# Taking the last row of the last expert's w2 past the slot outputs, straight into the output tiles

## The chip, the cores and the metric

The kernel runs on one core of a Trainium2 chip. The metric is the device time of one execution in microseconds (us). Before the change the median of three runs was 121.67 us (121.21 to 122.52).

## The reference, cut to what matters

The program is a linear attention with decay (the RWKV step), followed by a soft mixture of experts: every expert works on four "slots", each a weighted mean of all 3072 tokens, and every token gets back a weighted mean of the 32 slot outputs. The change lies in the second half:

```
logits = x @ phi                                  # 3072 x 32
d = exp(logits - max over tokens);  d /= sum over tokens
slot_input = (d.T @ x).reshape(E, S_per_e, D)     # E = 8, S_per_e = 4, D = 384
for e in range(E):
    h = maximum(slot_input[e] @ w1[e], 0)         # 4 x 1024
    slot_out[e] = h @ w2[e]                       # w2[e]: 1024 x 384
c = exp(logits - max over slots);  c /= sum over slots
out = c @ slot_out                                # 3072 x 384
```

The kernel leaves out the maxima, uses one table of exponentials for both softmaxes, and divides late: by `csr` (one over a slot's sum over the tokens) in the slot outputs, by `rsr` (one over a token's sum over the slots) in the output tiles.

## The kernel before, in words

**The attention** (lines 128 to 575) takes up the first 90 us of the trace. Its loop over 32 pieces also sends off the weights, under GpSimd's queue: `load_w` (lines 133 to 139) loads the eight experts' w1, then the eight w2, with a cast from float32 to bf16. `W_AT` says at which piece which load is issued. The last expert's w2 comes in three loads after the loop (lines 576, 577): rows y = 0 to 3, rows 4 to 6, row 7. A "row" y is a slab of 128 x 384: w2 is laid out as `(p y) d -> p y d`, so slab y holds the rows 8p + y of the matrix, one on each partition p.

**The experts' first layer** (lines 614 to 631) leaves relu(slot_input @ w1) in `h_sb`, for two groups g of four experts; an expert's slots are in a block of 32 rows of its own, 96 to 127 for the last one. Lines 646 to 650 transpose that to `hT`. **The second layer** is `second(g, experts)`: for each slab y, each half x of the 384 columns and each expert, one product of 128 x 32 weights with 128 x 192 of w2, added up in the two PSUM banks `SO` (Xb and Yb). TensorE runs it in the order in which w2 arrives: all of group 0, the first two experts of group 1, one filler product (`busy(1)`), then the last expert but one, then the last expert. `row_sums` (line 635) makes the tokens' sums, a product with one column for each tile, and `row_recip` (line 640) inverts them on VectorE. Then lines 671 and 672 scale the two halves of the slot outputs into `so`, one on VectorE, one on ScalarE.

**The output** (lines 675 to 704) is 24 tiles of 128 tokens x 384. `emit` makes a tile with one product, `LexpT` (the table of exponentials, slots on partitions, columns of the tile 24 apart) times `so`, and evicts it with a scaling by `rsr`, on VectorE for even tiles and ScalarE for odd ones; tiles 0 and 1 are made in two halves, one on each engine. The tiles use six PSUM banks in turn (`ob`: T1, T0, Ab0, Vb, Xb, Yb). They leave in nine transfers of `sizes = [1, 1, 2, 2, 2, 4, 4, 4, 4]` tiles. Transfers 0, 1, 2, 4, 6 and 8 are issued by SyncE (SP), transfers 3, 5 and 7 by GpSimd (POOL):

```
O((sp, pool)[gi % 2 if gi > 1 else 0].dma_start(out=out_v[:, i0:i, :], in_=o_s))
```

Each engine runs its instructions in the order of the program text (`O` keeps it). So TensorE does nothing for the output before the last slab of the last expert is in and `so` is scaled.

Of the kernel before, what the change touches and what calls it, by code (L numbers as in the profile page):

```python
# [9 lines left out]
def kernel(  # L10
# [14 lines left out]
    C = 128  # L25
    nC = S // C
    Nn, Dm = out.shape
    ES = moe_phi.shape[1]
    E = moe_w1.shape[0]
# [3 lines left out]
    nF = F // C  # L33
# [5 lines left out]
    nN = Nn // C  # L39
# [6 lines left out]
    f32 = mybir.dt.float32  # L46
    bf = mybir.dt.bfloat16
    i32 = mybir.dt.int32
    AF = mybir.ActivationFunctionType
    ALU = mybir.AluOpType  # L50

    def O(ins):
        return tc.keep_in_program_order(ins)

    pe, dve, act, pool, sp = nc.tensor, nc.vector, nc.scalar, nc.gpsimd, nc.sync

    big = ctx.enter_context(tc.tile_pool(name="big", bufs=1))
    cst = ctx.enter_context(tc.tile_pool(name="cst", bufs=1))
# [6 lines left out]
    EG = E // 2  # L65
    raw = [big.tile([128, 3 * RW], f32, name=f"raw{j}") for j in range(NR)]
    eW2 = nF * Dm
    w1_all = big.tile([128, E, nM, F], bf, name="w1_all")

    def w2_of(e):  # L70
        g, j = divmod(e, EG)
        return raw[1 + g][:].bitcast(bf)[:, j * eW2:(j + 1) * eW2].rearrange("p (y d) -> p y d", y=nF)
# [4 lines left out]
    T0 = psb.tile([128, 1024], bf, name="T0")  # L77
    T1 = psb.tile([128, 1024], bf, name="T1")
    Ab = psb.tile([128, 2, 512], f32, name="Ab")
# [13 lines left out]
    LexpT = cst.tile([128, Nn], bf, name="LexpT")  # L93
# [39 lines left out]
    def load_w(n, y0=0, y1=nF):  # L133
        if n < E:
            O(pool.dma_start(out=w1_all[:, n, :, :],
                             in_=moe_w1[n].rearrange("(p mo) f -> p mo f", p=128)))
        else:
            O(pool.dma_start(out=w2_of(n - E)[:, y0:y1, :],  # L138
                             in_=moe_w2[n - E].rearrange("(p y) d -> p y d", p=128)[:, y0:y1, :]))

    def keep_warm(n, bank=Yb, data=None):
        data = warm if data is None else data
        for _ in range(n):
            O(pe.matmul(bank[:, 0:512], data[:, 0:128], data[:, 0:512], start=True, stop=True))  # L144
# [349 lines left out]
    for i in range(-5, nH):  # L494
# [50 lines left out]
        if i in Z_AT:  # L545
            q = Z_AT[i]
# [12 lines left out]
        if i == 6:  # L559
            for mi in range(nM):  # L560
                for j in range(nM):
# [4 lines left out]
                                start=(j == 0), stop=(j == nM - 1)))  # L566
# [6 lines left out]
            load_w(nw)  # L573
            nw += 1
    assert nw == 2 * E - 1
    for y0, y1 in ((0, 4), (4, 7), (7, 8)):
        load_w(nw, y0, y1)


# [2 lines left out]
    Ab0 = Ab[:, 0, :]  # L582

    def busy(n):
        keep_warm(n, Ab[:, 1, :], w1_all[:, 0, 0, :])
# [23 lines left out]
    csr = cst.tile([128, 1], f32, name="csr")  # L609
# [4 lines left out]
    hb = [[Ab0, Vb[:]], [Yb[:], Ab[:, 1, :]]]  # L614
    FH = F // 2
    PH = C // 2
    h_sb = [Wf[0].bitcast(bf)[:, g * F:(g + 1) * F].rearrange("p (y c) -> p y c", c=C) for g in range(2)]
    hT = [Wf[1].bitcast(bf)[:, g * F:(g + 1) * F].rearrange("p (y c) -> p y c", c=C) for g in range(2)]
    for g in range(2):
        for a in range(2):  # L620
            for mi in range(nM):
                for j in range(EG):
                    O(pe.matmul(hb[g][a][32 * j:32 * j + 32, 0:FH], uns[:, mi, g, j, :],
                                w1_all[:, g * EG + j, mi, a * FH:(a + 1) * FH],
                                start=(mi == 0), stop=(mi == nM - 1), skip_group_check=True))
            src = hb[g][a][:, 0:FH].rearrange("p (q y) -> p y q", y=nF)
            dst = h_sb[g][:, :, a * PH:(a + 1) * PH]
            if a == 0:
                O(act.activation(out=dst, in_=src, func=AF.Relu))
            else:  # L630
                O(dve.tensor_scalar(out=dst, in0=src, scalar1=0.0, scalar2=None, op0=ALU.max))

    rsr = cst.tile([128, nN], f32, name="rsr")

    def row_sums(a, z):
        for i in range(a, z):
            O(pe.matmul(Mb[:, i:i + 1], LexpT[:, i:Nn:nN], ones[:, 0:1],
                        start=(i == a), stop=(i == z - 1), skip_group_check=True))

    def row_recip(a, z):  # L640
        O(dve.reciprocal(rsr[:, a:z], Mb[:, a:z]))

    HD = Dm // 2
    NY = nF // 2
    tb = [[T0[:], T1[:]], [Ab0.bitcast(bf), Vb[:].bitcast(bf)]]
    for g in range(2):
        for y in range(nF):
            O(pe.transpose(tb[g][y // NY][:, (y % NY) * C:(y % NY + 1) * C], h_sb[g][:, y, :], ident[:]))
        O(act.copy(hT[g][:, 0:NY, :].rearrange("p y c -> p (y c)"), tb[g][0][:, 0:NY * C]))
        O(dve.tensor_copy(hT[g][:, NY:nF, :].rearrange("p y c -> p (y c)"), tb[g][1][:, 0:NY * C]))  # L650
        if g == 0:
            row_sums(0, 8)
    row_recip(0, 8)
    SO = [Xb[:, 0:HD], Yb[:, 0:HD]]

    def second(g, experts):
        for y in range(nF):
            for x in range(2):
                for j in experts:
                    O(pe.matmul(SO[x][32 * j:32 * j + 32, :], hT[g][:, y, 32 * j:32 * j + 32],  # L660
                                w2_of(g * EG + j)[:, y, x * HD:(x + 1) * HD],
                                start=(g == 0 and y == 0), stop=(g == 1 and y == nF - 1), skip_group_check=True))

    second(0, range(EG))
    second(1, range(EG - 2))
    busy(1)
    second(1, (EG - 2,))
    second(1, (EG - 1,))
    row_sums(8, 12)
    so = Wf[1].bitcast(bf)[:, 2 * F + nM * ES * 8:2 * F + nM * ES * 8 + Dm]  # L670
    O(dve.tensor_scalar_mul(so[:, 0:HD], SO[0], csr[:, 0:1]))
# [7 lines left out]
             Wf[0][:, 2 * Dm:4 * Dm]]  # L679
            + [raw[0][:, x * 4 * Dm:(x + 1) * 4 * Dm] for x in range(4)])  # L680

    def emit(i, bank, dst, x0, x1, eng):
        op = ob[bank % 6][:, 0:x1 - x0]
        O(pe.matmul(op, LexpT[:, i:Nn:nN], so[:, x0:x1], start=True, stop=True))
        if eng is dve:
            O(dve.tensor_scalar_mul(dst[:, x0:x1], op, rsr[:, i:i + 1]))  # L686
        else:
            O(act.activation(out=dst[:, x0:x1], in_=op, func=AF.Copy, scale=rsr[:, i:i + 1]))

    i = 0  # L690
    for gi, sz in enumerate(sizes):
        o_s = obuf[gi][:, 0:sz * Dm].rearrange("p (n m) -> p n m", m=Dm)
        i0 = i
        for j in range(sz):
            if i < 2:
                emit(i, 2 * i, o_s[:, j, :], 0, HD, dve)
                emit(i, 2 * i + 1, o_s[:, j, :], HD, Dm, act)
            else:
                emit(i, i + 2, o_s[:, j, :], 0, Dm, (dve, act)[i % 2])
            i += 1  # L700
            if i in (6, 12):
                row_sums(i + 6, i + 12)
                row_recip(i + 6, i + 12)
        O((sp, pool)[gi % 2 if gi > 1 else 0].dma_start(out=out_v[:, i0:i, :], in_=o_s))  # L704
# [30 lines left out]
```

The softmax here doesn't subtract the row's maximum and nothing guards it: scores larger than these inputs give would overflow.

## Time and profile before

| | |
|---|---|
| median of three runs | 121.67 us (121.21 to 122.52) |
| the profiled execution, its time | 121.55 us |
| the profiled execution, its span | 119.8 us |
| mean granted TensorE clock | 0.959 |
| busy: TensorE, VectorE, ScalarE, GpSimd | 102.0, 96.4, 83.9, 59.2 us |
| last piece of w2 on chip | 103.1 us |
| first output transfer issued | 104.74 us |
| last output eviction done | 110.87 us |
| output data stops moving | 117.5 us |

How to read it: the span is what the profile covers, 1.75 us less than the time of the same execution. A time "at 103.1 us" is counted from the start of the span. The profile's page gives busy time by engine, the span in 40 slices, the transfers by queue (q0: those that GpSimd issues, q1: those of SP and ScalarE), and the chain of work that ended last. The timeline lists instructions with their start, duration, engine, line, output and inputs; `SPq` and `POOLq` are the engines' instruction sequencers, and "issue to landing" is the time from a transfer's instruction to its completion.

### The profile page before, as it was taken

The page shows a single profiled execution, that of the slowest core. Times are in us where ns is not written, and L with a number is a line of the kernel's source. Part 1 is how long each engine was busy: PE and PEld are TensorE (multiplying, and loading weights), DVE is VectorE, ACT ScalarE, POOL GpSimd, SP SyncE. Part 2 cuts the span into 40 slices and gives each one's busy share as a digit, 9 for nine tenths or more (in the row PEclk, how much of TensorE's full clock was granted, in tenths as well). Part 3 has the DMA queues.
Part 4 walks back from the last instruction along what each step waited for, and adds up shares of the span by engine and source line. Part 5 has one row for each costly group of instructions (what it writes and reads, how often), then busy time and mean ns, then how long its engine had stood idle before and what let it go on. Part 6 is the DMA issues. An engine that isn't in the chain of part 4 may idle for free.

```text
span 119.8 us, 4336 instructions
## 1 busy us (share of the span) xinstructions
PE 102.0 (85%) x1797; PEld 82.0 (68%) x1797; DVE 96.4 (81%) x187; ACT 83.9 (70%) x183; POOL 59.2 (49%) x70
## 2 busy tenths in 40 slices
PE   5994977799999999999999999999998998896000
PEld 1453866687888888889878798888785696683000
DVE  6899999999999999899999899999954420399000
ACT  4459769797988898988988997998882520398000
POOL 7328634599999999788677595011000000013000
PEclk9998699999999999999999999999999999999955
DMA  2999999999999999999999999999999998179992
GB/s 83 255 370 374 373 367 369 363 391 367 339 381 385 348 229 215 213 213 217 213 217 213 217 218 215 212 217 212 217 215 217 211 209 161 23 274 383 410 410 99
DMA packets 20925, 31.79 MB, mean 265 GB/s; under 512 B 1129, under 2 KB 17898, under 8 KB 20906
## 3 DMA queue, kind: packets, MB, share of 16 engines
q0 software_dynamic: 2960, 14.55, 55.5%
q1 hardware_dynamic: 17920, 16.96, 41.8%
q8 instruction: 14, 0.23, 0.7%
q14 instruction: 5, 0.04, 0.1%
q10 hardware_dynamic: 26, 0.00, 0.0%
HBM read 39.38 MB, written 4.72 MB: 368 GB/s over the span
## 4 chain that ended last, share of the span: by engine, by line
DMA 34%; PE 28%; DVE 17%; issue 6%; ACT 3%; POOL 3%; POOLq 0%; DVEq 0%; ACTq 0%
DMA raw<-in_moe_w_dram 34%; PE Vb L284 4%; PE T L235 3%; DVE W L188 3%; DVE prod L257 3%; PE Ab L299 3%; PE Yb L352 2%; POOL kr L228 2%; DVE AT L304 2%; PE T L247 2%; PE Mb L325 2%; DVE kn L252 2%; DVE Z L341 2%; PE Yb L144 2%; PE Yb L365 1%
## 5 line engine op out<-in xcount | busy, mean ns | idle before, releaser
L228 POOL TENSOR_TENSOR kr<-raw,W 128x576 bf16<-128x576 f32 x30 | 42.2, 1428 | 13.8 <-ACT W L192 6.2
L304 DVE TENSOR_TENSOR AT<-Ab,mask_ut 128x768 bf16<-128x768 f32 x32 | 30.3, 946 | 0.8 <-PE Ab L299 0.6
L235 PE MATMUL T<-ident,kr 128*128 128x128 bf16 x192 | 16.8, 227 | 1.8 <-POOL kr L228 1.7
L284 PE MATMUL Vb<-v_bf,Q 128*128 128x96 bf16 x288 | 17.8, 208 | 0.0
L284 PEld LDWEIGHTS <-Q 128*128 128x128 bf16 x288 | 15.9, 99 | 1.5 <-issue 0.2
L241 ACT COPY kT<-T 128x768 bf16<-128x768 bf16 x16 | 12.8, 800 | 4.6 <-PE T L235 3.3
L241 ACT COPY rT<-T 128x768 bf16<-128x768 bf16 x16 | 12.8, 801 | 4.2 <-PE T L235 3.6
L257 DVE TENSOR_TENSOR prod<-T,kT 128x768 bf16<-128x768 bf16 x16 | 15.2, 948 | 0.0
L235 PEld LDWEIGHTS <-kr 128*128 128x128 bf16 x192 | 12.5, 101 | 2.6 <-POOL kr L228 1.9
L342 DVE TENSOR_TENSOR dv<-vn,Mb 128x288 bf16<-128x288 bf16 x32 | 14.1, 440 | 0.0
L290 ACT CAST vn<-Vb 128x288 bf16<-128x288 f32 x32 | 13.4, 419 | 0.1
L341 DVE TENSOR_TENSOR Z<-Mb,zt 128x288 bf16<-128x288 f32 (+1 forms) x32 | 12.7, 397 | 0.6
L372 ACT CAST x<-Yb 128x288 bf16<-128x288 f32 x32 | 13.1, 409 | 0.1
L299 PE MATMUL Ab<-rT,kT 64*128 64x128 bf16 x192 | 11.1, 222 | 2.1 <-DVE AT L304 2.0
L704 POOL DMA_DIRECT2D out_dram<-W x1 | 0.6, 552 | 24.2 <-DVE W L686 24.2
L325 PE MATMUL Mb<-vn,kn 128*128 128x96 bf16 (+2 forms) x80 | 11.5, 242 | 0.0
L352 PE MATMUL Yb<-vn,AT 128*128 128x48 bf16 x192 | 10.3, 185 | 0.1
L270 ACT CAST v_bf<-raw 128x576 bf16<-128x576 f32 x15 | 10.2, 678 | 0.0
L299 PEld LDWEIGHTS <-kT 64*128 64x128 bf16 x192 | 5.6, 95 | 5.6 <-DVE AT L304 2.0
L352 PEld LDWEIGHTS <-AT 128*128 128x128 bf16 x192 | 7.1, 96 | 3.3
L138 POOL DMA_DIRECT2D raw<-in_moe_w_dram x10 | 5.5, 558 | 7.8 <-DMA raw<-in_moe_w_dram 7.7
L365 PE MATMUL Yb<-dv,ident 128*128 128x288 bf16 x32 | 9.1, 284 | 0.2
(143 smaller groups left out, 221.3 us busy)
## 6 DMA issues: line engine op xcount, KB each, us to landing
w_all<-in_moe_w_dram POOLq DMA_DIRECT2D x8, 768.0 KB, 12.9
raw<-in_moe_w_dram POOLq DMA_DIRECT2D x7, 768.0 KB, 18.2
raw<-in_v_dram SPq DMA_DIRECT2D x12, 288.0 KB, 6.6
raw<-in_k_dram SPq DMA_DIRECT2D x8, 288.0 KB, 6.0
raw<-in_r_dram SPq DMA_DIRECT2D x8, 288.0 KB, 6.2
raw<-in_k_dram SPq DMA_DIRECT2D x2, 1152.0 KB, 12.3
raw<-in_r_dram SPq DMA_DIRECT2D x2, 1152.0 KB
out_dram<-raw POOLq DMA_DIRECT2D x2, 768.0 KB, 6.9
```

Source lines behind the costliest of these rows:

```text
L228: O(eng.tensor_mul(kr[:, j].rearrange("p j (h s) -> p j h s", s=64)[:, :, :, 0:D], src, W[j][:, q].rearrange("p j (h d) -> p j h d", h=2)))
L235: O(pe.transpose(bank[:, x * C:(x + 1) * C], kr[:, j, x, :], ident[:]))
L241: O(act.copy(t[:].rearrange("p (s j) -> p s j", j=J), bank[:, 0:S].rearrange("p (j s) -> p s j", j=J)))
L257: O(dve.tensor_mul(pr[:].rearrange("p (s j) -> p s j", j=J), T1[:, 0:S].rearrange("p (j s) -> p s j", j=J), st["kT", m][:].rearrange("p (s ...
L284: O(pe.matmul(Vb[:, c * P2:(c + 1) * P2], Q3[:, o:o + C], vb[:, :, g, j, :], start=(j == 0), stop=(j == JV - 1)))
L290: O(act.copy(vn[:].rearrange("p c e d -> p (c e d)"), Vb[:, 0:L * P2]))
L299: O(pe.matmul(Ab[:, e, c * C:(c + 1) * C], kT[s, t], rT[s, t]))
L304: O(dve.tensor_mul(AT[:], Ab[:, :, 0:T].rearrange("p e (c t) -> p e c t", c=L), mask_ut[:, None, None, :].to_broadcast([128, 2, L, C])))
L325: O(pe.matmul(o, kn[:, g * L + c, :], vc, start=first, stop=True, skip_group_check=True))
L341: O(dve.tensor_mul(Z[:], Mb[:, 0:x * P2].rearrange("p (c e) -> p c e", c=x), zt[:, q, 0:x, :]))
L342: O(dve.tensor_mul(dv[:], st["v", i][:].rearrange("p c e d -> p (c e) d"), Mb[:, 288:288 + 2 * L, None].to_broadcast([128, L * 2, D])))
L352: O(pe.matmul(Yb[:, o:o + D], AT[:, e, c, :], vn[:, c, e, :], start=first, stop=False, skip_group_check=True))
```

## The change

Row y = 7 of the last expert no longer goes through `second`, `SO` and `so`. Its part of an output tile is LexpT(tile)^T · (hs · w2[7]), where hs holds the hidden values of that slab, scaled by `csr`. The product is made in the other order: ahead of time (hs^T · LexpT), a 128 x 128 block for each tile, called `gl`; and then, for each tile, gl times the slab w2[7], added in the tile's PSUM bank to the product with `so`.

- `hs_half` (two instructions on ScalarE) makes hs from the first layer's PSUM banks.
- `g_last(q)`, six times, makes `gl` for four tiles: one product with 512 columns on TensorE, whose moving operand is LexpT read with a step of 24 columns, and one eviction of 128 x 512, on ScalarE for even q, on VectorE for odd q. Four stand between the pieces of the second layer, in the place of `busy(1)` and after; numbers 4 and 5 stand in the output loop after four and after eight tiles. `gl` is kept in the last expert's w1, which is used up by then.
- `emit` issues two products for a tile. For tiles 0 and 1 the four `gl` products come first, ahead of the loop.
- The last expert's w2 is loaded in four pieces instead of three.

```diff
-    for y0, y1 in ((0, 4), (4, 7), (7, 8)):
+    for y0, y1 in ((0, 4), (4, 6), (6, 7), (7, 8)):
         load_w(nw, y0, y1)
...
+    last = slice(32 * (EG - 1), 32 * EG)
+    hs = cst.tile([128, C], bf, name="hs")
+
+    def hs_half(a):
+        O(act.activation(out=hs[last, a * PH:(a + 1) * PH], in_=hb[1][a][last, nF - 1:FH:nF], func=AF.Relu,
+                         scale=csr[last, 0:1]))
+
+    hs_half(0)
+    gl = w1_all[:, E - 1, :, :].rearrange("p m f -> p (m f)")
+    GB = 4
+    gbank = [Ab[:, 1, :], T0[:].bitcast(f32), T1[:].bitcast(f32), Ab0, Ab[:, 1, :], Ab[:, 1, :]]
+
+    def g_last(q):
+        O(pe.matmul(gbank[q].rearrange("p (i t) -> p i t", t=C), hs[last, :],
+                    LexpT[last, :].rearrange("p (t i) -> p i t", i=nN)[:, q * GB:(q + 1) * GB, :],
+                    start=True, stop=True))
+        dst = gl[:, q * GB * C:(q + 1) * GB * C]
+        if q % 2:
+            O(dve.tensor_copy(dst, gbank[q]))
+        else:
+            O(act.copy(dst, gbank[q]))
...
+    hs_half(1)
     row_recip(0, 8)
...
-    def second(g, experts):
-        for y in range(nF):
+    def second(g, experts, ys=range(nF)):
+        for y in ys:
...
-                                start=(g == 0 and y == 0), stop=(g == 1 and y == nF - 1), skip_group_check=True))
+                                start=(g == 0 and y == 0),
+                                stop=(g == 1 and y == nF - 1 - (j == EG - 1)), skip_group_check=True))
 
     second(0, range(EG))
     second(1, range(EG - 2))
-    busy(1)
+    g_last(0)
     second(1, (EG - 2,))
-    second(1, (EG - 1,))
+    g_last(1)
+    g_last(2)
+    second(1, (EG - 1,), range(0, 4))
+    g_last(3)
+    second(1, (EG - 1,), range(4, nF - 1))
     row_sums(8, 12)
...
-    def emit(i, bank, dst, x0, x1, eng):
+    def emit(i, bank, dst, x0, x1, eng, first=True, then=True):
         op = ob[bank % 6][:, 0:x1 - x0]
-        O(pe.matmul(op, LexpT[:, i:Nn:nN], so[:, x0:x1], start=True, stop=True))
+        if first:
+            O(pe.matmul(op, gl[:, i * C:(i + 1) * C], w2_of(E - 1)[:, nF - 1, x0:x1], start=True, stop=False))
+        if not then:
+            return
+        O(pe.matmul(op, LexpT[:, i:Nn:nN], so[:, x0:x1], start=False, stop=True))
...
+    for i in range(2):
+        for x in range(2):
+            emit(i, 2 * i + x, None, x * HD, (x + 1) * HD, None, then=False)
     i = 0
...
-                emit(i, 2 * i, o_s[:, j, :], 0, HD, dve)
-                emit(i, 2 * i + 1, o_s[:, j, :], HD, Dm, act)
+                emit(i, 2 * i, o_s[:, j, :], 0, HD, dve, first=False)
+                emit(i, 2 * i + 1, o_s[:, j, :], HD, Dm, act, first=False)
             else:
                 emit(i, i + 2, o_s[:, j, :], 0, Dm, (dve, act)[i % 2])
             i += 1
+            if i in (4, 8):
+                g_last(3 + i // 4)
             if i in (6, 12):
                 row_sums(i + 6, i + 12)
                 row_recip(i + 6, i + 12)
```

## The prediction

> **What bounds the kernel now.** I read the chain of waits first, then the timeline from 101 us, then the busy times by stretch with their DMA rates. The chain over the last third begins:
>
> ```profile
> 77.84 24.80 DMA raw<-in_moe_w_dram
> 102.64 0.04 issue
> 102.68 0.24 PE Xb L660
> ...
> 103.46 0.43 DVE W L671
> ...
> 103.93 0.33 PE T L684 x2
> ```
>
> The load of w2 (issued 77.84, landed 102.64) sets the end of the second layer. The piece with row 7 was issued at 81.91 and took 21.2 us, so it landed at 103.1, just as TensorE came to it (103.17). The timeline shows the handover to the output:
>
> ```profile
> 103.17 0.25 PE L660 MATMUL Xb<-raw,W 128*32 128x192 bf16 x1
> 103.43 0.44 PE L637 MATMUL Mb<-ones,LexpT 128*128 128x1 bf16 x4
> 103.46 0.42 DVE L671 TENSOR_SCALAR W<-Xb,csr 128x192 bf16<-128x192 f32 x1 [6.40 <-PE Xb L660]
> 103.93 0.33 PE L684 MATMUL T<-W,LexpT 128*128 128x192 bf16 x2
> 104.21 0.42 DVE L686 TENSOR_SCALAR raw<-T,rsr 128x192 f32<-128x192 f32 x1
> 104.74 0.36 SPq L704 DMA_DIRECT2D out_dram<-raw  x1
> ```
>
> From the landing of row 7 to the first output eviction there are 1.1 us. From there the stretches (length, busy time of PE, PEld, DVE, ACT, POOL, clock, DMA share, GB/s) say what rules:
>
> ```profile
> 105.00:105.50 0.50, 0.50 (x9) 0.49 (x7) 0.50 (x2) 0.50 (x3) 0.00 (x0) 1.00 0.00 0
> 105.50:106.00 0.50, 0.50 (x5) 0.46 (x5) 0.50 (x2) 0.50 (x3) 0.00 (x0) 1.00 0.78 280
> 107.50:108.00 0.50, 0.46 (x3) 0.28 (x2) 0.50 (x3) 0.50 (x2) 0.00 (x0) 1.00 0.99 363
> 109.50:110.00 0.50, 0.33 (x2) 0.00 (x0) 0.50 (x2) 0.50 (x2) 0.00 (x0) 1.00 1.04 381
> 117.00:117.50 0.50, 0.00 (x0) 0.00 (x0) 0.00 (x0) 0.00 (x0) 0.00 (x0) 0.50 0.97 393
> ```
>
> The DMA engines are silent until 105.6, then full until 117.5. The last 7.7 us of it are data alone: 16 tiles of 196,608 bytes, 0.483 us each at the mean of some 407 GB/s after 110. Afterwards 2.3 us remain to the span's end. So the end is set by the start of the output's data, *as long as tiles are handed over fast enough*. They hardly are. GpSimd's transfers:
>
> ```profile
> 106.60 0.55 POOL L704 DMA_DIRECT2D out_dram<-W  x1 [24.16 <-DVE W L686]
> 108.22 0.53 POOL L704 DMA_DIRECT2D out_dram<-raw  x1 [1.06 <-ACT raw L688]
> ```
>
> In 0.1 us stretches of the DMA view the first's packets (q0) appear at 108.7 (2.1 us after issue), just as q1 runs dry; the second's at 109.8 (1.6 us after), a tenth after the first has run out. SP's first transfer moves 0.86 us after issue. The second line (tiles 8 to 11, evicted by 107.65, issued 0.57 later) has no margin: what delays tile 11 delays everything.
>
> **What the Trainium skill says.** "TensorE: Matmul & The Clock Gate", section "Wait — 56ns, not 53.3ns?", prices a matmul at N / 2.4 GHz plus 2.5 ns: 162.5 ns for 384 columns. The trace agrees (L684 at 105.58, 105.75, 105.91, 106.07). "SBUF — State Buffer", section "Door 1: The DMA port swizzle", says that stepping past a 16-byte line at each access (over 8 bf16) pays a penalty, without a figure. `g_last` steps by 24. The trace has that step only in weight loads: L637's row sums start 0.068 us apart, the packed loads of L426 0.025. "DMA: Bandwidth & Descriptors", section "Specifications", gives a first byte after about 1 us from GpSimd, 0.6 from SP; the trace says 1.6 to 2.1, and 0.86.
>
> **The change, part by part.**
>
> *The loads.* One more piece on POOL. The last two issues each waited for an earlier w2 load (77.84, 81.91); a third such wait gives about 85.6, with nothing queued on POOL behind it before 106. Bytes and order stay. From 101.35 to 102.64 three rows came in, then one in 0.46: 0.43 to 0.46 each, with no visible price for a piece. So rows 4 and 5 land at 102.2, row 6 at 102.65, row 7 at 103.1. Extra descriptors might add 0.1; below nothing isn't possible with the same bytes.
>
> *hs.* Two ScalarE instructions of 32 x 64. The nearest rows evict 192 in 0.42 and 384 in 0.59, so at most 0.4 each. ScalarE is idle 94.91 to 95.28, and after 96.88: hidden. Uncovered, the first would push L649 and so `hT` by 0.1, into TensorE's wait for w2.
>
> *Four `g_last` ahead of the output.* 512 columns cost 0.216 packed (384 cost 0.163) and 0.27 at the weight loads' strided price (4 x 0.068). I take 0.24; the other end, a doubled 0.43, is a rival. Number 0 replaces the filler. Numbers 1 and 2 start at 100.8, where TensorE waits to 101.39: done by 101.28, hidden. Number 3 follows rows 0 to 3 at 102.04, ends by 102.28, rows 4 and 5 by 102.6, and row 6 runs at its landing, 102.69. Its eviction on VectorE (about 0.66) runs 102.5 to 103.15, ahead of L671, which could start at 102.95. So the scaling goes 103.15 to 103.55 instead of 103.46 to 103.88. The sums (0.28), then four `gl` halves of 0.081 from 103.2, fill TensorE till 103.53.
>
> *The start.* First product with `so` at 103.6 instead of 103.93: **0.33 us gained** at the first eviction and the first transfer (104.41).
>
> *The output loop.* Each tile from number 2 takes two products of 0.163, 0.326 in all. Before, evictions ruled: ScalarE takes a tile every 0.47, VectorE every 0.52, together 0.25 a tile. Now TensorE rules. Up to the end of tile 11 it issues four halves (0.32), 20 products (3.26), two `g_last` (0.48) and six row sums (0.35, from 105.00 to 105.38): 4.42 us. From 103.6 that is 108.02. Tile 11's last product starts at 107.86, its eviction 0.36 later (0.28 at L684's first half, 0.08 for twice the columns) and takes 0.59: **108.81 instead of 107.65, 1.16 later**. The two `gl` evictions (0.6 ScalarE, 0.66 VectorE) come ahead of tiles 5 and 10, 0.6 us late at tile 5, but both engines have caught up by tile 11.
>
> *The drain.* Tiles 0 to 3 are out by 107.3. Tiles 6 and 7 (SP, about 107.3) move from 108.2, tiles 4 and 5 (POOL, 107.1 plus 2.1) after them: 0.9 us empty. Tiles 8 to 11 are issued at 108.81 + 0.57 = 109.38 and move from 110.96 instead of 109.8: 0.8 empty. What follows (tiles 12 to 15 issued at 110.5, 16 to 19 at 112.3) arrives before its turn. So the end moves by 1.16, the early start being inside that sum. 121.55 + 1.16 = 122.7 for the profiled execution; the median was 0.12 above it: **122.8 us**.
>
> **Rivals.**
>
> *Shorter POOL latency.* If 109.8 was ring order behind tiles 4 and 5, and the latency is nearer the page's 1 us, tiles 8 to 11 move at 110.43 (109.38 + 1.05), 0.63 later than now: 122.3. Against: 1.6 is already the shortest seen; the first w1 load took 2.5 (issue 38.88, q0 packet after 41.4).
>
> *Strided reads cost double or more.* At 0.43, the loop's two add 0.38. Ahead of it, rows 0 to 3 start at 101.66, row 6 ends at 103.24, number 3's eviction ends at 103.6, L671 at 104.03: products start 0.48 later than forecast. 1.16 + 0.38 + 0.48 = 2.0: 123.7. For: the page's penalty. Against: 0.068 for 128 strided columns.
>
> *No early scaling.* Pieces 6 and 7 land together, or L671 waits: start as before, 123.2.
>
> *Not slower.* The output stays fed, and the early start is kept: 121.67 - 0.33 = 121.3. It decides at tiles 8 to 11: evicted by 107.32, 1.5 us before my sum, that is with `gl` products nearly free. TensorE needs 0.41 a tile there on average, the data 0.483, which speaks for it; batches of four tiles plus POOL's latency speak against.
>
> **How the numbers follow.** Forecast 0.52 (own range 122.4 to 123.2), shorter latency 0.17, strided 0.15, no early scaling 0.07, not slower 0.09. The range 121.7 to 123.8 leaves out the "not slower" case and a strided price above double. One per cent, about what a measurement of this kernel can tell from no change, ends at 122.9: half of the forecast (0.26), all of strided (0.15) and most of "no early scaling" (0.06) are slower, 0.47; 0.03 of "not slower" is faster; the remaining 0.50 are the same.
>
> **What would show it.** Right: first output transfer near 104.4; tile 11 evicted near 108.8; TensorE busy without gaps to about 112, evictions waiting for it; two DMA gaps between 107 and 111. Wrong: `g_last` above 0.3 us, L671 at 103.4 or later, POOL packets under 1.3 us after issue, or a DMA share that never drops between 106 and 118.

## The result, and the profile after

The changed kernel takes 127.82 us in the median of six runs (127.1 to 128.77), the kernel before, run beside it, 121.48 us: a ratio of 1.0518, 95% interval 1.0446 to 1.059. It is slower by 6.3 us where 1.2 was forecast, and lies outside the range. The profiled execution took 128.41 us with a span of 126.6; it is one of the three upper ones of the six runs (127.1, 127.2, 127.2, 128.4, 128.7, 128.8), so sums from the trace come out some 0.6 above the median. In what follows a ratio leaves out runs more than 1.5 per cent above the fastest of the same kernel (one each of two experiments, and four of the kernel before), while a median has all runs.

The timeline of the changed kernel at the handover, to be read beside that of before:

```profile
99.11 1.04 PE L647 MATMUL Ab<-LexpT,hs 32*128 32x512 bf16 x1
101.51 1.93 PE L647 MATMUL T<-LexpT,hs 32*128 32x512 bf16 x2
104.13 1.04 PE L647 MATMUL Ab<-LexpT,hs 32*128 32x512 bf16 x1
106.07 0.42 DVE L700 TENSOR_SCALAR W<-Xb,csr 128x192 bf16<-128x192 f32 x1 [0.17 <-PE Xb L684]
107.02 0.52 PE L717 MATMUL T<-W,LexpT 128*128 128x192 bf16 x2
107.48 0.42 DVE L719 TENSOR_SCALAR raw<-T,rsr 128x192 f32<-128x192 f32 x1 [0.70 <-PE T L717]
108.03 0.84 SPq L742 DMA_DIRECT2D out_dram<-raw  x2
```

A `g_last` product (L647) holds TensorE for 0.97 us (the next instruction's start, 100.08, less 99.11), 0.88 when two follow each other (1.93 less 1.05), where 0.24 was put down. Four of them, in the waits for w2, overrun these waits: the scaling of the slot outputs starts at 106.07 (103.46 before, 103.15 forecast), the first output transfer is issued at 108.03 (104.74 before, 104.41 forecast). No TensorE instruction waits for w2 there any more.

The chain of waits has changed hands. In its last part it names no transfer of w2, and TensorE's own work follows itself:

```profile
99.18 0.97 PE Ab L647
...
101.58 1.86 PE T L647 x2
...
104.20 0.97 PE Ab L647
...
108.95 0.97 PE Ab L647
...
111.49 0.63 DVE W L719
112.16 1.04 PE Ab L647
```

Six `g_last` make 5.8 us of this chain. The last one waited for an eviction (L719). The stretches (columns as before) add two things:

```profile
106.00:106.50 0.50, 0.50 (x7) 0.38 (x6) 0.42 (x1) 0.27 (x1) 0.00 (x0) 0.50 0.00 0
112.00:112.50 0.50, 0.34 (x1) 0.00 (x0) 0.11 (x1) 0.33 (x1) 0.20 (x1) 1.00 0.00 0
115.00:115.50 0.50, 0.50 (x5) 0.36 (x4) 0.35 (x2) 0.23 (x1) 0.00 (x0) 1.00 0.00 0
116.00:116.50 0.50, 0.50 (x5) 0.36 (x4) 0.50 (x1) 0.43 (x2) 0.08 (x1) 1.00 0.00 0
117.00:117.50 0.50, 0.50 (x5) 0.36 (x4) 0.47 (x2) 0.50 (x1) 0.00 (x0) 1.00 1.01 418
124.00:124.50 0.50, 0.00 (x0) 0.00 (x0) 0.00 (x0) 0.00 (x0) 0.00 (x0) 0.50 0.69 271
```

The granted clock is 0.50 at 106, and it is so from 105.2 to 108.6; in the kernel before it was 1.00 through this part. And the DMA engines stand still near 112 and from 115 to 116.5, with the next tiles not yet handed over. The transfer of tiles 8 to 11 is issued at 115.55, moves from 116.6, and the output's data stop at 124.35.

### The profile page after: what moved, and what is told of

Its sections match the earlier page's. It is cut to its first block, busy times and chain, and to the rows that moved or that the text cites. A ratio compares the mean times of both kernels' runs of the same rounds, so it can differ in the third digit from the quotient of the medians.

```text
span 126.6 us, 4407 instructions
## 1 busy us (share of the span) xinstructions
PE 111.4 (88%) x1825; PEld 85.1 (67%) x1826; DVE 99.5 (79%) x190; ACT 87.0 (69%) x188; POOL 60.2 (48%) x71
## 4 chain that ended last, share of the span: by engine, by line
PE 65%; DVE 16%; ACT 8%; issue 4%; POOL 1%; DVEq 0%; ACTq 0%
PE T L235 7%; PE Vb L284 6%; PE Ab L299 5%; DVE prod L257 4%; PE Yb L352 4%; DVE AT L304 4%; PE Yb L144 3%; PE Ab L647 3%; PE Mb L325 3%; PE T L247 3%; PE Xb L684 2%; DVE dv L342 2%; PE Yb L365 2%; PE Yb L684 2%; PE Xb L380 2%
## 5 line engine op out<-in xcount | busy, mean ns | idle before, releaser
L138 POOL DMA_DIRECT2D raw<-in_moe_w_dram x11 | 6.0, 555 | 10.5 <-DMA raw<-in_moe_w_dram 5.8
```

## The experiments

Theory S: what costs is that the moving operand of `g_last` steps by 24 columns. Rival T: it is the two products for each tile, and the waits of the output loop. Each ratio below is to the kernel before on the same chip, with its 95% interval.

**Packed reads.** The change with one edit:

```diff
-        O(pe.matmul(gbank[q].rearrange("p (i t) -> p i t", t=C), hs[last, :],
-                    LexpT[last, :].rearrange("p (t i) -> p i t", i=nN)[:, q * GB:(q + 1) * GB, :],
-                    start=True, stop=True))
+        O(pe.matmul(gbank[q], hs[last, :], LexpT[last, q * GB * C:(q + 1) * GB * C], start=True, stop=True))
```

> Only the moving operand of the six g_last products is changed: 512 neighbouring columns of LexpT in place of columns 24 apart, so the gl blocks hold the tokens in another order and row 7's part goes to the wrong tokens; every instruction, size, bank and wait stays. Theory S (the step of 24 in the moving operand is what costs): a product falls from 0.97 to about 0.22 us, row 6 runs at its landing near 102.7, the clock stays whole, the first output transfer is issued near 104.4 and the time is about 122.7, where the forecast had it. Rival T (two products for each tile and the waits in the output loop are what costs): the time stays above 125.

Measured: 123.19 us, 1.0103 (1.0058 to 1.0148). Its row for `g_last` (minimum, median and maximum in ns, first and last start):

```profile
L647 PE MATMUL Ab<-LexpT,hs x4: 371/378/385, 99.1 to 107.5; 32*128 32x512 bf16 x4
```

378 ns in place of 1040; the first transfer leaves at 104.57; the clock stays at 1.00 until TensorE's work is done. No other edit was made, and four fifths of the loss are gone, what the fall of the clock cost among them (an estimate of that is in the next part). T falls as the main cause.

**Without `g_last`.** The function returns at once; the output loop keeps its two products.

```diff
     def g_last(q):
+        return
```

> The six g_last products and their evictions are left out; gl then holds the last expert's w1, so row 7's part is wrong, but the output loop still issues two products for each tile and the loads and hand-over are those of the change. Theory S: start as in the forecast (first transfer near 104.4), TensorE needs 0.48 us less up to tile 11 than in the forecast, so about 122.3. Rival T: this keeps the double products, so above 125.

Measured: 121.82 us, 0.9988 (0.9968 to 1.0009). That is 0.5 us under what I expected. Two products for each tile and the fourth load piece, with row 7 taken past the scaling, are a draw with the kernel before. In the profiled execution row 6 ran only at 103.05, so the first transfer, at 104.75, was no earlier than before.

**`g_last` alone.** The kernel before with hs, the six products and their evictions at the change's places, and nothing that reads them:

```diff
-    busy(1)
+    g_last(0)
     second(1, (EG - 2,))
-    second(1, (EG - 1,))
+    g_last(1)
+    g_last(2)
+    second(1, (EG - 1,), range(0, 4))
+    g_last(3)
+    second(1, (EG - 1,), range(4, nF))
...
+            if i in (4, 8):
+                g_last(3 + i // 4)
```

> The kernel before, with hs and the six g_last products (step of 24) and their evictions added at the places that they have in the change; gl is never read, row 7 goes through the slot outputs as before, one product for each tile, three load pieces. Theory S: nearly the whole loss is here: first output transfer near 107.9, two more products of 0.97 in the loop, about 127 in all. Rival T: 0.9 us at the most for the start and the loop, 122 to 123.5.

Measured: 126.69 us, 1.0401 (1.0341 to 1.0461), first transfer at 107.24. Packed reads take 4.15 points off the loss of the whole change, and the six products alone make a loss of 4.0: nearly the whole loss is there without anything that reads their result.

**The halves.** The four products ahead of the output strided and the two in the loop packed, and the reverse:

```diff
+        if q in (4, 5):                 # the reverse: (0, 1, 2, 3)
+            O(pe.matmul(gbank[q], hs[last, :], LexpT[last, q * GB * C:(q + 1) * GB * C], start=True, stop=True))
+        else:
...
```

> The change, with the two late g_last products (numbers 4 and 5) reading 512 neighbouring columns; the four ahead of the output keep the step of 24. The token order of gl is wrong for tiles 16 to 23. If the loss ahead of the output adds to that in the loop: start as in the change (first transfer near 108), then as with packed reads, 126 to 126.5 where packed reads gave 123.2. If one hides behind the other: 127.5 or more, or 124 or less.

> The opposite half: the four g_last products ahead of the output read neighbouring columns, the two in the output loop keep the step of 24. Token order of gl wrong for tiles 0 to 15. If the parts add: first transfer near 104.5, two products 0.75 us longer each, both ahead of tiles 8 to 11: 124.5 to 125. If the loop's strided products hide behind the evictions and the transfers: 123.2 to 123.6.

Measured: 126.61 us (125.65 to 128.15), 1.0335 (1.0247 to 1.0423), and 124.59 us, 1.019 (1.0132 to 1.0248). Over packed reads the four ahead add 2.3 points and the two in the loop 0.9. Both parts count, about as forecast; together they give 4.2 per cent, a point under the change's 5.2, which these intervals don't exclude. In the profiled execution of the second half w2 came late, and the first transfer left at 105.24, not near 104.5; it is the slowest of that half's four runs.

**The price of the step by itself.** A ladder of products behind the last output product of the kernel before: groups of eight, one group for each step, with six packed products of 512 columns (`filler`) ahead of each group. The group at step 8:

```diff
+    filler(6)
+    for _ in range(8):
+        O(pe.matmul(Ab[:, 1, 0:128], warm_w[0:128, :], LexpT[0:128, 0:1024:8], start=True, stop=True))
```

> The kernel before, and after its last output product a ladder on TensorE: groups of eight products with a moving operand of 128 columns of LexpT, 1, 2, 4, 8, 12, 16 or 24 columns apart, on 128 rows and then on 32 rows, six packed products of 512 between the groups; then four products of 512 in the order of g_last (four runs of 128 with a step of 24) on 128 rows, four that also write PSUM with a step, and four that read runs of four neighbours, 24 apart. Nothing reads the results. If the price is that of the memory line (theory S, line of 16 bytes), steps 1 to 4 cost 0.056 us for 128 columns or little more, and from step 8 on each costs the same 0.24 us as g_last shows (0.97 for 512), whatever the rows; runs of four neighbours cost about a quarter of the surplus, 0.4 us for 512. If the price grows with the distance instead, step 24 costs more than step 8. If it is the 32 rows that cost, 128 rows are cheap.

From its timeline, one row for a group: steps 1, 4, 8 and 24 with 128 columns, then 512 columns in `g_last`'s order, then 512 in runs of four neighbours:

```profile
111.62 0.61 PE L714 MATMUL Ab<-LexpT,ident 128*128 128x128 bf16 x8
115.12 1.08 PE L720 MATMUL Ab<-LexpT,ident 128*128 128x128 bf16 x8
117.33 1.97 PE L723 MATMUL Ab<-LexpT,ident 128*128 128x128 bf16 x8
126.71 1.95 PE L732 MATMUL Ab<-LexpT,ident 128*128 128x128 bf16 x8
149.34 3.71 PE L756 MATMUL Ab<-LexpT,ident 128*128 128x512 bf16 x4
159.03 1.05 PE L762 MATMUL Ab<-LexpT,ident 128*128 128x512 bf16 x4
```

A group's length, less one product's own duration, over the seven (or three) steps between starts, is the price of one: 0.056 us at step 1, 0.057 at step 2, 0.112 at step 4, 0.224 at step 8, 0.221 at step 24. On 32 rows step 24 costs 0.222. So the price doubles from step 2 to step 4 (8 bytes), doubles again at step 8 (16 bytes) and stays there; 32 rows cost what 128 cost. In `g_last`'s order 512 columns cost 0.88, whether PSUM is written packed or with a step (0.88), and 0.22 in runs of four: reading four neighbours and then jumping costs nothing extra. I had expected step 4 to be nearly free and the runs of four at 0.4; both were off.

**A packed version that computes everything.** `gl` in the tokens' own order with packed reads, all six products ahead (with banks and evicting engines to suit), the step of 24 moved to the weight loads:

```diff
-        O(pe.matmul(op, gl[:, i * C:(i + 1) * C], w2_of(E - 1)[:, nF - 1, x0:x1], start=True, stop=False))
+        O(pe.matmul(op, gl[:, i:Nn:nN], w2_of(E - 1)[:, nF - 1, x0:x1], start=True, stop=False))
```

> A version that computes the whole reference: gl is made in the tokens' own order with packed reads, all six products ahead of the output loop in TensorE's waits for w2, and the step of 24 moves to the weight loads of gl in the output loop, where a load of 128 such columns takes 0.155 us behind a product of 0.163. Theory S: six products of 0.22 hide in the waits, first transfer near 104.4, and tile 11 comes about 0.7 us later than before because of the double products: 122.1 to 122.3. Rival T: no better than 125. If the second strided weight load for each tile doesn't hide, some 0.05 to 0.1 us for each tile is added: 123 to 124.

Measured: 122.39 us, 1.0033 (1.0015 to 1.0052). The strided weight loads do hide (between the row sums the loop's products start 0.163 us apart). The six products don't quite: rows 0 to 3 run at 102.03, after five of them, and the first transfer leaves at 105.22, 0.5 later than before, not at 104.4.

**Runs of four.** The smallest repair: the change's places, banks and evictions, `g_last` reading four neighbours at a time, and the weight loads of `gl` in `emit` stepping by 4 to fit (that line is not shown).

```diff
-        O(pe.matmul(gbank[q].rearrange("p (i t) -> p i t", t=C), hs[last, :],
-                    LexpT[last, :].rearrange("p (t i) -> p i t", i=nN)[:, q * GB:(q + 1) * GB, :],
+        O(pe.matmul(gbank[q].rearrange("p (t i) -> p t i", i=GB), hs[last, :],
+                    LexpT[last, :].rearrange("p (t i) -> p t i", i=nN)[:, :, q * GB:(q + 1) * GB],
```

> The change with its g_last products reading runs of four neighbouring columns, 24 apart, in the order tokens outside, tiles inside, and gl's weight loads stepping by 4; six products, evictions, banks and places as in the change, and the whole reference is computed. The ladder showed 0.24 us for 512 columns read so, against 0.93 in the change's order: the time should be that of packed reads, 1.0 per cent above the kernel before (123.2). If a step in the weight loads or the 32 rows matter: above 124.

Measured: 123.46 us, 1.0132 (1.0095 to 1.0169), the same as packed reads within their intervals. What is left, 1.0 to 1.3 per cent, is the rest of the change.

**The hand-over of the output.** One edit, on the kernel before and on the version in the tokens' order:

```diff
-        O((sp, pool)[gi % 2 if gi > 1 else 0].dma_start(out=out_v[:, i0:i, :], in_=o_s))
+        O(sp.dma_start(out=out_v[:, i0:i, :], in_=o_s))
```

> The kernel before with all nine output transfers issued by SyncE. If the output's data already flow without a gap (as I read the profile of before), the later start of GpSimd's transfers cost nothing: 0 to 0.3 us faster. If the gaps near 108.9 and 109.7 count: 0.3 to 0.6 faster. If one queue moves less than two in turn: slower.

> The version with gl in the tokens' order and packed reads, all products ahead (e4), with all nine output transfers issued by SyncE. It still computes the whole reference. If the late hand-over through GpSimd (0.57 us from eviction to issue, 1.6 from issue to the first packet) is what leaves the DMA engines empty in the changed output loop, tiles 8 to 11 move about 0.9 us earlier and the time falls by 0.5 to 0.9 below e4's, to that of the kernel before or a little under it. If production on TensorE is what is late, it gains under 0.3.

Measured: the kernel before becomes 0.9949 (0.9926 to 0.9971) of itself, and 0.9944 (0.9921 to 0.9966) when run again beside the next experiment; the other becomes 0.9975 (0.9957 to 0.9994), 0.6 per cent under its own figure with GpSimd.

> The kernel before with all output transfers on SyncE once more, on the same chip as e11: 0.5 per cent faster than the kernel before.

The reason isn't only the one expected. In the profiled executions the data of the kernel before stop at 117.5 with GpSimd and 117.3 without; but the span then ends 1.6 us after that instead of 2.3. In all four executions with SyncE alone it ends 1.6 us after the data, in the nine timed ones with GpSimd, before and after among them, 2.2 to 2.3. Of the 1.3 us by which the version in the tokens' order shrinks (span 120.6 to 119.3), 0.5 are data stopping earlier, the rest is this tail. Part of it comes back outside the span: a run's time less its span is 2.05 to 2.15 us in the mean of each of the four experiments with SyncE alone, and 1.8 in those with GpSimd. So of the 0.7 of the tail some 0.4 are gained. What GpSimd does in the tail no run shows.

**Late products on SyncE's version.** As the runs of four, all transfers on SyncE, numbers 4 and 5 moved behind tiles 12 and 14:

```diff
-            if i in (4, 8):
-                g_last(3 + i // 4)
...
+            if i in (12, 14):
+                g_last(i // 2 - 2)
```

> As e10, with all nine output transfers on SyncE and the two late g_last products moved behind tiles 12 and 14, after the transfer of tiles 8 to 11. Start as with packed reads (first transfer near 104.6), tile 11 evicted near 108.5 and moving near 109.5, where the eight tiles before it run out at 109.3: the early start is kept, 0.2 us faster than the kernel before with its transfers on SyncE, 0.7 per cent faster than the kernel before. If the double products still cost more than the early start gains: as e9 or slower, 0.2 per cent faster.

Measured: 122.88 us, 1.0101 (1.0053 to 1.0149): a miss. The timeline at tile 12:

```profile
108.42 0.39 PE L647 MATMUL Ab<-LexpT,hs 32*128 32x512 bf16 x1
108.85 0.59 ACT L654 CAST w_all<-Ab 128x512 bf16<-128x512 f32 x1
109.48 0.32 PE L714 MATMUL Ab<-raw,w_all 128*128 128x384 bf16 x1 [0.67 <-ACT w_all L654]
```

Tile 12 goes to the first bank of `Ab`, `g_last` had written the second, and yet tile 12 waits 0.67 us for the eviction of the second. The next `g_last` then waits 0.44 for tile 12's eviction. The two banks are one tile in the program, and these waits go by the tile. `gl`, which that eviction writes and tile 12 reads, is not the reason: in the changed kernel tile 4's product reads `gl` at 109.85, while an eviction writes other columns of it from 109.95 to 110.54. Up to there all went as planned (tiles 8 to 11 were issued at 108.78 and the data ran without a gap to 111.5); then they stand still for over 1.5 us.

## Why the prediction was wrong, point by point

**The step that failed** is "Four `g_last` ahead of the output": "512 columns cost 0.216 packed … and 0.27 at the weight loads' strided price … I take 0.24". It is a mis-sized term in a mechanism that had a name: "Strided reads cost double or more" was a rival, at 0.43. It measured 0.88 back to back and 0.97 alone. I had carried a price from one operand to the other: weight loads of 128 columns with this step start every 0.068 us, while a moving operand takes 0.22 for as many columns. A row of another instruction was no bound from above, and the range, cut at "double", was too narrow for that reason. (In that rival's sum 104.03 is where L671 ends, not where it starts.) A second term, the clock, was put at nothing.

**What it did to the sum.** Ahead of the output, four products of 0.9 and more stand where a filler of 0.2 and waits of 0.4 and 0.5 were to make room: rows 0 to 3 run at 103.37 instead of 101.39, and the scaling comes 2.9 us after the forecast. In the loop two more, 0.7 each over the forecast, all ahead of tiles 8 to 11. That both parts count, the two halves show. How much each weighs can be read from three places in the changed kernel, and the same three with packed reads: the product behind the fourth `g_last`, the fifth `g_last`, the issue of tiles 8 to 11 (three lines of the changed kernel, then three of packed reads).

```profile
105.10 0.29 PE L684 MATMUL Xb<-raw,W 128*32 128x192 bf16 x1
108.88 1.04 PE L647 MATMUL Ab<-LexpT,hs 32*128 32x512 bf16 x1
115.55 0.53 POOL L742 DMA_DIRECT2D out_dram<-raw  x1 [3.35 <-ACT raw L721]
...
102.51 0.26 PE L682 MATMUL Xb<-raw,W 128*32 128x192 bf16 x1
104.87 0.37 PE L647 MATMUL Ab<-LexpT,hs 32*128 32x512 bf16 x1
110.20 0.53 POOL L740 DMA_DIRECT2D out_dram<-raw  x1 [2.68 <-ACT raw L719]
```

Tiles 8 to 11 are issued 5.35 us later. The four products ahead make 2.6 of that (105.10, not 102.51), the two in the loop 1.3 (6.67 from the fifth product to the issue, not 5.33). The remaining 1.4 arise between the fourth and the fifth, where the same instructions take 3.78 instead of 2.36.

**The clock** is what differs there, and it was not in my sum at all. From 105.2 to 108.6 products took twice as long (0.16 for 192 columns in the chain, 0.08 before). So the half clock cost some 1.4 us in this execution, an estimate from these two traces. The six times of the changed kernel lie in two groups as far apart (127.1 to 127.2, 128.4 to 128.8), and the profiled execution, where the clock fell, is of the upper. That the clock held in the lower one fits, but is not shown: no trace of it was kept, and the mean granted clocks (0.967 to 0.970, and 0.957 to 0.972) don't tell the groups apart. The strided half ahead spreads likewise (125.65, 125.86, 127.36, 128.15); its profiled execution, where the clock fell, took 127.36.

Why the clock fell is open. It fell while output products were still to come in the three kernels with four strided products ahead: in this one; with the strided half ahead, at 105.5; and with `g_last` alone, only at 110.1, after the first of the two in its loop. In the others, the strided half in the loop among these, it held from the second layer until TensorE's last product was done. But the step by itself is not enough. The ladder ran 72 products at a step of 8 or more, eight of them in `g_last`'s own order with 512 columns, four in a row, and its clock stayed at 1.00:

```profile
111.00:160.00 49.00, 48.57 (x220) 20.59 (x222) 0.33 (x1) 0.00 (x0) 0.36 (x1) 1.00 0.15 59
```

There the products of 512 ran on 128 rows, with packed products of 128 rows between the groups; in the change they ran on 32 rows, with narrow ones of 32 weight columns between them. Which of this matters was not tried. "TensorE: Matmul & The Clock Gate", Part 1, in the Trainium skill has the clock go to half after at least one idle window of about 3.4 us. The 3.4 us for which it stayed at half here agree with one window in length, but TensorE was busy in every tenth of a us from 102.0 to 105.2, so idleness as the profile counts it doesn't explain the fall.

**The output loop**: two products of 0.16 for each tile, TensorE ahead of the evictions as what rules, were right. What I missed is the wait through `Ab` (0.46 us for the last `g_last`, in the change and with packed reads).

**GpSimd's latency** was read wrongly. I took 1.6 to 2.1 us from issue to first packet, and found the Trainium skill's figure of about 1 us ("DMA: Bandwidth & Descriptors", "Specifications") to differ. With the DMA engines empty, the changed kernel shows 1.05 (111.65 to 112.7, 115.55 to 116.6), packed reads 1.05 as well (110.20 to 111.25): the page was right. In the kernel before the DMA engines were busy with other output data until these packets began (108.7) or until 0.1 before (109.7), so they most likely stood behind others. My rival "shorter POOL latency" had it.

**The total with packed reads** is what the forecast described, 1.2 us slower; it measured 1.0103, 1.26 us. But that it agrees so well is luck, since two errors cancel in it: tiles 8 to 11 were issued 0.8 later than forecast (110.20, not 109.38), and moved 0.5 sooner after issue.

**Right**: the fourth piece of w2, issued at 85.11 and hidden; hs, 0.31 for each instruction and hidden; the evictions of `gl`, 0.59 and 0.69; gaps in the output's data ahead of tiles 8 to 11; and that the early scaling, even where it worked (packed reads, 104.57), is lost again in the loop.

## What to carry to other kernels

Before an operand is read with a step, price it for the side on which it is read. The step of 24 that hid in the weight loads cost four times the packed price as a moving operand here, and the order could be turned so that the step came to the weights, or so that four neighbours were read at a time. Before work is put into an engine's waits, compare it with the length of these waits at the upper price, not at the hoped-for one. Moving a product off the longest chain is worth what the chain is shortened by, less what is then paid for each tile; here 0.3 us were to be gained against twice the products for each tile, a draw at best.

## What the runs showed of the hardware that was not expected

- A moving bf16 operand was read at full rate at steps of 1 and 2 elements, at half rate at 4, at a quarter from 8 to 24 (0.056, 0.057, 0.112, 0.224, 0.221 us for 128 columns), on 32 rows as on 128. Runs of four neighbours, 24 apart, cost nothing extra (0.22 us for 512). In the Trainium skill "SBUF — State Buffer", "Door 1: The DMA port swizzle", gives 8 bf16 as how far one can step for free; for a moving operand the ladder differs, with half the rate at 4.
- The granted clock can fall to 0.50 for 3.4 us while the profile counts TensorE as busy throughout, at an estimated cost of 1.4 us. It did so behind strided products of 32 rows in three kernels, and not in the ladder, where as slow ones ran in a row; what sets it off is open.
- Without output transfers on GpSimd's queue the span ended 1.6 us after the last data, with them 2.2 to 2.3; some 0.3 of the difference came back outside the span. The kernel before with that one edit, 0.5 and 0.6 per cent faster in two comparisons, is the best version found, and it doesn't need the change.
